# Token-weight transposes in two 64-row halves, own priorities for loads and for every operation

## Chip, cores and metric

The kernel runs on one core of a Trainium2 chip. The metric is the device time of one execution in microseconds (us), median of the runs shown. One execution was also taken by the hardware profiler; its page and trace give where the time goes.

## What is computed

A linear recurrence over the sequence (state of 40 x 40 for each of 4 x 8 batch-heads, 768 steps), and a phase mixer on its output.

```python
# recurrence, for each step t:
y[:, :, t] = einsum('bhd,bhde->bhe', rt, state)
Sa = einsum('bhde,bhe->bhd', state, at)
state = state * wt[:, :, None, :] - einsum('bhd,bhe->bhde', Sa, bt) \
        + einsum('bhd,bhe->bhde', vt, kt)
# mixer on x = y as (batch 4, 768 tokens, 320 channels):
theta = x @ w_theta
zr, zi = x * cos(theta), x * sin(theta)
u = x + einsum('ts,bsd->btd', w_tok_r, zr) + einsum('ts,bsd->btd', w_tok_i, zi)
out = u + maximum(u @ w_ch, 0)
```

## The kernel before

**Tiles.** The sequence is cut into chunks of 128 tokens: 6 chunks in each of 4 batches, 24 tiles `i`. For a tile, the recurrence is done in chunk form for all eight heads at once, with heads padded from 40 to 64 columns so that a pair of heads fills 128.

**Stages of a tile.** `loads` issues five loads on SyncE's queue (w, k, b, a, v, 160 KB each) and, for every second tile, r in two loads. `prep` takes the logarithm of w (ScalarE), its cumulative sum (TensorE) and the exponential of that (`ex`), multiplies k, b and a with it, converts v (GpSimdE, for the first two tiles VectorE and ScalarE) and transposes them on TensorE, ScalarE copying out. `attention_scores` makes three blocks of scores (`spsi`, `sphi`, `slv`), each by eight matmuls of 64 rows into a pair of PSUM banks (line 522), masked by VectorE (line 527). `recurrence` carries the state (`x0`, `nu`, `gt`), `readout` makes a fourth block of scores (`slu`) and the output `x`, `theta` multiplies by w_theta.

**Mixer.** When a batch's six tiles are done, `sines` takes cosine and sine (ScalarE, with a table switch) and GpSimdE multiplies with x into `zr` and `zi`. `mix_row` (line 724) then makes one row block of 128 tokens out of 12 matmuls with 320 columns; VectorE adds x, three transposes, three matmuls with w_ch, VectorE's last step, and a store.

**Token weights.** Both 768 x 768 token matrices are needed transposed. `wtok_block(tb)` (lines 760 to 779), for six blocks of 128 rows, loads the rows of `w_tok_r` and of `w_tok_i` by GpSimdE's queue into `wrow` (two buffers each), and for each matrix runs one TensorE operation `wt` of six 128 x 128 transposes into a single PSUM bank, and one VectorE copy `ewt` into `wtok`.

**Order.** Nothing is issued in program order. Every operation is added to a plan with its engine, an estimated cost, the buffers that it reads and writes, and a tag; `Plan.order` then simulates the engines and at each step issues, for an engine, the ready operation with the lowest score: its priority plus `WAIT` times how much later it could start than the earliest candidate, plus `TSWITCH` for a change of ScalarE's table. The priority is a time for the tile or row (`TIMES`) plus an offset for the kind of operation (`OFF`), line 77. A load of token weights is not planned before its release time (`rel`, in us; the entry 2 + `tb`). TensorE work has a mode, 128 or 64 rows, and the plan adds time for changing it (`INTO64`, `OUTOF64`). The eight PSUM banks are planned too: four as two pairs (cumulative sums and scores), four singly (all else). Buffers `raw_w`, `raw_a`, `raw_kb` and `raw_v` have four copies each, by tile number (lines 287 to 303).

Of the kernel before, what the change touches and what calls it, by code (L numbers as in the profile page):

```python
# [9 lines left out]
FP32 = mybir.dt.float32  # L10
# [10 lines left out]
FREE0 = {"PE": 800.0, "ACT": 2100.0, "DVE": 4400.0, "POOL": 3600.0, "SP": 740.0}  # L21
BANKS = 8
DOUBLE = 4
INTO64, OUTOF64 = 95.0, 120.0
SP_DEPTH = 3600.0

# [7 lines left out]
class Plan:  # L34
# [34 lines left out]
    def link(self):  # L69
        ops = self.ops  # L70
        users = {}
        for o in ops:
            o.succ = []
            o.npre = len(o.pre)
            o.start = o.end = None
            o.banks = None
            o.prio = 1000.0 * (TIMES[o.spec[0]][o.spec[1]] + OFF[o.spec[2]])
            for k in set(o.reads) | set(o.writes):
                if k[0] == "ps":
                    users.setdefault(k, set()).add(o)  # L80
        for o in ops:
            o.soft = set()
            if o.new is not None and not o.loose:
                u = users[o.new[0]]
                o.soft = {p for x in u if x is not o for p in x.pre if p not in u}
                o.soft -= set(o.pre)
            o.npre += len(o.soft)
        for o in ops:
            for p in o.pre:
                p.succ.append(o)  # L90
            for p in o.soft:
                p.succ.append(o)
        return users

    def order(self):
# [44 lines left out]
        while len(out) < n:  # L140
            pick = None
            for e, lst in ready.items():
                if not lst:
                    continue
                te = free[e]
                if e == "SP":
                    te = max(te, dma - SP_DEPTH)
                cand = []
                lo = None
                for o in lst:  # L150
                    t = max(te, est0[o])
                    b = None
                    if o.new is not None:
                        f = find(o)
                        if f is None:
                            continue
                        t = max(t, f[0])
                        b = f[1]
                    if e == "PE" and o.mode != mode:
                        t = max(t, te + (INTO64 if o.mode == 64 else OUTOF64))  # L160
                    cand.append((t, o, b))
                    if lo is None or t < lo:
                        lo = t
                if lo is None:
                    continue
                best = None
                for t, o, b in cand:
                    s = o.prio + WAIT * (t - lo)
                    if e == "ACT" and o.table is not None and o.table != table:
                        s += TSWITCH  # L170
                    if best is None or (s, o.idx) < best[0]:
                        best = ((s, o.idx), t, o, b)
                if pick is None or best[1] < pick[1]:
                    pick = best
# [48 lines left out]
def mm(n):  # L223
    return max(n / 2.4 + 2.5, 25.0)


def tail(n):
# [1 line left out]


OFF = dict(
    ah=-14.03, ch=37.4, cs=-41.22, ea=-6.95, egd=-90.74, egt=-28.2, ekb=21.31, enu=-16.72,
    enut=-11.56, er=-13.46, eth=-25.65, eut=-58.98, ev=17.32, ewt=-9.73, ex=39.26, exp=-63.71,
    ext=-55.21, gd=7.06, gt=16.39, kb=36.69, ln=-32.13, load=-20.04, loadr=-19.62, mlu=62.71,
    mlv=10.93, mphi=44.82, mpsi=69.12, nu=-17.14, nut=12.45, nx=-78.15, oo=13.49, r=35,
    row=38.73, sin=86.83, slu=-15.77, slv=39.92, sphi=-32.67, spsi=-35.87, st=34.23, ta=1.11,
    th=36.56, tkb=-1, tr=0.69, tv=4.86, uadd=-6.95, ut=37.54, v=-26.35, wdma=123.77, wt=37.8,
    x0=-27.08, xt=21.68, y=-40.12, z=24.68)
WAIT, TSWITCH = 435.08, 606442.0
TIMES = dict(  # L240
    tile=[
        -61.22, -38.55, -36.31, -3.78, 3.05, 10.64, 15.26, 42.47, 45.62, 46.74, 54.55, 58.02,
        77.61, 85.12, 102.64, 108.62, 104.48, 129.91, 135.62, 135.6, 150.73, 158.77, 165.34,
        174.78],
    row=[
        47.97, 37.38, 30.67, 33.44, 59.07, 74.74, 77.47, 97.12, 115.85, 115.75, 105.42, 129.53,
        141.42, 164.22, 173.87, 137.03, 124.06, 133.88, 191.51, 200.6, 184.9, 268.51, 279.77,
        212.96],
    rel=[
        -48.76, 34.55, 63.09, 65.85, -76.89, 92.41, 33.44, 33.52])  # L250


@with_exitstack
def kernel(
# [29 lines left out]
    def sb(name, shape, dt, n):  # L284
        return [consts.tile(shape, dt, name=f"{name}_{i}") for i in range(n)]

    raw_w = sb("raw_w", [128, H, D], FP32, 4)
    raw_a = sb("raw_a", [128, H, D], FP32, 4)
    raw_kb = sb("raw_kb", [128, 2, H, D], FP32, 4)
    raw_v = sb("raw_v", [128, H, D], FP32, 4)  # L290
    raw_r = sb("raw_r", [128, 2, 8 * D], FP32, 2)

    def load(i):
        bi, ci = divmod(i, NCH)
        s = i % 4

        def src(ap):
            return ap[bi, :, ci * C:(ci + 1) * C, :].rearrange("h t d -> t h d")
        return ([("raw_w", s), raw_w[s], src(w)],
                [("raw_k", s), raw_kb[s][:, 0], src(k)],  # L300
                [("raw_b", s), raw_kb[s][:, 1], src(b)],
                [("raw_a", s), raw_a[s], src(a)],
                [("raw_v", s), raw_v[s], src(v)])

    ident = consts.tile([128, 128], BF16, name="ident")
    mask_p = consts.tile([128, 1, 128], BF16, name="mask_p")
# [73 lines left out]
    def ps(key):  # L380
        h = plan.home[key]
        return doubles[h[0] // 2] if len(h) == 2 else singles[h[0] - DOUBLE]

# [3 lines left out]
    def add(eng, kind, i, fn, cost, reads=(), writes=(), at="tile", **kw):  # L387
        return plan.add(eng, kind, i, fn, cost, tuple(reads), tuple(writes),
                        (at, i, kind), **kw)
# [23 lines left out]

    def loads(i):
        for key, dst, src in load(i):
            add("SP", "load", i,
                lambda dst=dst, src=src: nc.sync.dma_start(out=dst, in_=src),
                650, [], [key], work=1030)
        bi, ci = divmod(i, NCH)
        if ci % 2 == 0:  # L420
            rr = r[bi, :, ci * C:(ci + 2) * C, :].rearrange(
                "(c g) (t q) d -> c t g (q d)", c=2, q=8)
            s = i // 2 % 2
            for c in range(2):
                add("SP", "loadr", i,
                    lambda c=c: nc.sync.dma_start(out=raw_r[s][:, c], in_=rr[c]),
                    600, [], [("raw_r", s, c)], work=520)

    def natural(t):
        return t.rearrange("p (c g) d -> p g c d", c=2)  # L430

    def paired(t):
        return t.rearrange("p (g c) d -> p g c d", c=2)

    def prep(i):
# [30 lines left out]
        for j, nm in enumerate("kb"):  # L466
# [3 lines left out]
                490 if fast else 864, [("raw_" + nm, s4), kex], [("kb", j, i % NKB)])  # L470
        add("DVE" if fast else "POOL", "ah", i,
            lambda: (nc.vector if fast else nc.gpsimd).tensor_tensor(  # L472
                out=paired(ah)[:, :, :, 0:D], in0=natural(raw_a[s4]), in1=Wi, op=ALU.mult),
            490 if fast else 864, [("raw_a", s4), kex], [("ah", i % 3)])
        copy = nc.scalar.copy if fast else nc.gpsimd.tensor_copy
        add("ACT" if fast else "POOL", "v", i,
            lambda: copy(out=paired(vb)[:, :, :, 0:D], in_=natural(raw_v[s4])),
            460, [("raw_v", s4)], [("v", i % NRV)])
        def tr(kind, kinde, srcs, dst, skeys, dkey, eng):
            p = ("ps", kind, i)  # L480
            n = 4 * len(srcs)
# [278 lines left out]
    def wtok_block(tb):  # L760
        i = 7 + tb
        for nm, ap in (("r", moe_w_tok_r), ("i", moe_w_tok_i)):
            row = wrow[nm][tb % 2]
            add("POOL", "wdma", 2 + tb, lambda row=row, ap=ap: nc.gpsimd.dma_start(
                out=row, in_=ap[tb * 128:(tb + 1) * 128, :]), 580, [],
                [("wrow", nm, tb % 2)], at="rel", work=1240, release=2 + tb)
            p = ("ps", "wt" + nm, tb)

            def go(row=row, p=p):
                t = ps(p).bitcast(BF16)  # L770
                for s in range(NT):
                    nc.tensor.transpose(out=t[:, s * 128:(s + 1) * 128],  # L772
                                        in_=row[:, s * 128:(s + 1) * 128], identity=ident)
            add("PE", "wt", i, go, 6 * mm(128), [("wrow", nm, tb % 2)], [p], new=(p, 1),
                tail=tail(128))
            add("DVE", "ewt", i, lambda nm=nm, p=p: nc.vector.tensor_copy(
                out=wtok[nm][:, :, tb * 128:(tb + 1) * 128],
                in_=ps(p)[:, 0:384].bitcast(BF16).rearrange("p (a b) -> p a b", b=128)),
                550, [p], [("wtok", nm, tb)])

    def mix_rows(bi):
# [71 lines left out]
```

## Time and profile before

| | |
|---|---|
| median of 4 runs | 216.05 us (215.3 to 216.66) |
| profiled execution | 216.33 us |
| its span, first to last instruction | 214.6 us |
| TensorE clock granted | 1.00 throughout |
| token-weight transposes (line 772) | 72 of 128 x 128, from 74.1 to 116.7 us |
| token-weight loads, issued | 66.9 to 107.6 us, in 12 issues |
| first row matmul (line 724) | 76.3 us |
| tile loads | last raw_v issued at 163.1 us |

The longest waits of VectorE, GpSimdE and ScalarE and where they end (engine, line waited for: total us, times, longest):

```profile
POOL kb L468 <- ACT ex L460: 32.8, 9, 15.7
ACT uT L401 <- PE ps_s L625: 17.0, 15, 4.5
POOL zr L706 <- ACT cs L694: 12.8, 6, 5.1
DVE u L734 <- PE ps_s L724: 11.1, 15, 1.3
```

How to read it: PE is TensorE, PEld its weight loads, DVE VectorE, ACT ScalarE, POOL GpSimdE, SP SyncE; a q after the name means the sequencer or queue of that engine. "A <- B" says that A stood idle until B had ended. "ps_s" is a single PSUM bank, "ps_d" a pair. The matmuls of TensorE are pipelined: the duration of one is several times the step from one to the next.

### The profile page before, as it was taken

What the parts mean: (1) busy time and instruction counts of PE and PEld (TensorE: products, weight loads), DVE (VectorE), ACT (ScalarE), POOL (GpSimd) and SP (SyncE); (2) the same over time, 40 slices, a digit from 0 to 9 for tenths busy, and PEclk for the clock granted to TensorE, in tenths of its full rate; (3) what the DMA queues carried; (4) which work ended last, traced back from release to release, by engine and by line L of the source; (5) the groups of instructions that cost most, each with busy time, mean ns of one, the idle gap of its engine ahead of it and who ended that gap; (6) DMA issues with size and microseconds to landing.
All of it is one profiled execution on the core that took longest, in us unless ns stands there. A gap on an engine that the chain in (4) does not pass through costs nothing.

```text
span 214.6 us, 8107 instructions
## 1 busy us (share of the span) xinstructions
PE 195.5 (91%) x3344; PEld 156.4 (73%) x3344; DVE 165.6 (77%) x252; ACT 148.7 (69%) x340; POOL 117.4 (55%) x173
## 2 busy tenths in 40 slices
PE   1478789897999999999999999999999999999993
PEld 1366678685787787888878888787888888777771
DVE  7247798779879798968987889978979899744533
ACT  4266676799989969968788756589967996642101
POOL 5000657488667797967589225386667587150000
PEclk9999999999999999999999999999999999999999
DMA  6999989989898999974999999888999110011222
GB/s 100 212 165 181 165 152 176 185 176 164 176 175 179 185 154 207 192 126 98 210 182 200 175 154 185 144 162 193 159 183 185 34 35 3 0 34 63 91 95 92
DMA packets 134181, 30.82 MB, mean 144 GB/s; under 512 B 125824, under 2 KB 134144, under 8 KB 134144
## 3 DMA queue, kind: packets, MB, share of 16 engines
q1 hardware_dynamic: 131712, 27.54, 65.7%
q0 software_dynamic: 2432, 2.77, 8.7%
q8 instruction: 26, 0.43, 0.8%
q14 instruction: 11, 0.09, 0.2%
HBM read 29.13 MB, written 3.93 MB: 154 GB/s over the span
## 4 chain that ended last, share of the span: by engine, by line
PE 77%; DVE 7%; DMA 4%; issue 3%; POOL 3%; ACT 2%; SPq 1%; POOLq 0%; DVEq 0%; ACTq 0%
PE ps_s L724 19%; PE ps_s L398 13%; PE ps_d L522 11%; PE ps_s L670 9%; PE ps_s L625 4%; DMA raw_a<-in_a_dram 3%; PE ps_s L573 3%; PE ps_s L505 3%; PE ps_s L591 3%; DVE phi L527 2%; PE ps_s L654 2%; DVE psi L527 2%; PE ps_s L772 2%; PE ps_s L652 2%; DMA raw_v<-in_v_dram 2%
## 5 line engine op out<-in xcount | busy, mean ns | idle before, releaser
L468 POOL TENSOR_TENSOR kb<-raw_kb,ex 128x320 bf16<-128x320 f32 x44 | 37.4, 865 | 34.4 <-ACT ex L460 32.8
L724 PE MATMUL ps_s<-zr,wtok_r 128*128 128x320 bf16 x144 | 40.7, 299 | 0.0
L724 PE MATMUL ps_s<-zi,wtok_i 128*128 128x320 bf16 x144 | 40.6, 299 | 0.0
L527 DVE TENSOR_TENSOR psi<-ps_d,mask_p 128x1024 bf16<-128x1024 f32 x24 | 29.2, 1218 | 7.3 <-PE ps_d L522 7.2
L527 DVE TENSOR_TENSOR lamu<-ps_d,mask_p 128x1024 bf16<-128x1024 f32 x24 | 29.3, 1220 | 4.7 <-PE ps_d L522 4.2
L527 DVE TENSOR_TENSOR lamv<-ps_d,mask_p 128x1024 bf16<-128x1024 f32 x24 | 29.0, 1217 | 3.0 <-PE ps_d L522 2.9
L527 DVE TENSOR_TENSOR phi<-ps_d,mask_n 128x1024 bf16<-128x1024 f32 x24 | 29.2, 1215 | 0.7 <-PE ps_d L522 0.6
L472 POOL TENSOR_TENSOR ah<-raw_a,ex 128x320 bf16<-128x320 f32 x22 | 19.0, 865 | 16.0 <-ACT ex L460 7.7
L706 POOL TENSOR_TENSOR zr<-cs,x 128x320 bf16<-128x320 f32 x23 | 17.8, 793 | 12.9 <-ACT cs L694 12.8
L460 ACT ACTIVATE ex<-ps_d 128x648 f32<-128x648 f32 x24 | 17.2, 717 | 7.6 <-PE ps_d L456 4.6
L734 DVE TENSOR_TENSOR u<-ps_s,x 128x320 bf16<-128x320 f32 x24 | 11.7, 488 | 11.2 <-PE ps_s L724 11.1
L401 ACT COPY uT<-ps_s 128x192 f32<-128x192 f32 x24 | 7.7, 321 | 17.1 <-PE ps_s L625 17.0
L706 POOL TENSOR_TENSOR zi<-cs,x 128x320 bf16<-128x320 f32 x23 | 17.7, 792 | 2.1 <-ACT cs L694 2.0
L522 PE MATMUL ps_d<-aT,kbT 64*128 64x128 bf16 x384 | 17.2, 221 | 1.1 <-DVE psi L527 0.5
L401 ACT COPY kbT<-ps_s 128x512 f32<-128x512 f32 x24 | 14.3, 595 | 4.6 <-PE ps_s L398 3.9
L724 PEld LDWEIGHTS <-wtok_r 128*128 128x128 bf16 x144 | 14.0, 97 | 4.5
L724 PEld LDWEIGHTS <-wtok_i 128*128 128x128 bf16 x144 | 14.1, 98 | 3.5
L398 PE MATMUL ps_s<-ident,kb 128*128 128x128 bf16 x192 | 15.4, 223 | 1.3 <-DVE kb L468 1.3
L743 DVE SCALAR_TENSOR_TENSOR oo<-ps_s,u 128x320 f32<-128x320 f32 x24 | 11.5, 486 | 5.2 <-PE ps_s L670 5.2
L654 PE MATMUL ps_s<-kb,lamu 128*128 128x40 bf16 x192 | 15.0, 180 | 0.5 <-DVE lamu L527 0.4
L522 PEld LDWEIGHTS <-kbT 64*128 64x128 bf16 x384 | 11.6, 96 | 5.2 <-issue 2.3
L652 PE MATMUL ps_s<-kb,lamv 128*128 128x40 bf16 x192 | 15.4, 180 | 0.0
(113 smaller groups left out, 556.6 us busy)
## 6 DMA issues: line engine op xcount, KB each, us to landing
raw_w<-in_w_dram SPq DMA_DIRECT2D x24, 160.0 KB, 3.9
raw_kb<-in_k_dram SPq DMA_DIRECT2D x24, 160.0 KB, 4.2
raw_kb<-in_b_dram SPq DMA_DIRECT2D x24, 160.0 KB, 4.2
raw_a<-in_a_dram SPq DMA_DIRECT2D x24, 160.0 KB, 4.2
raw_v<-in_v_dram SPq DMA_DIRECT2D x24, 160.0 KB, 3.9
raw_r<-in_r_dram SPq DMA_DIRECT2D x24, 160.0 KB, 3.7
out_dram<-oo SPq DMA_DIRECT2D x24, 160.0 KB, 2.1
wrow_r<-in_moe_w_tok_r_dram POOLq DMA_DIRECT2D x6, 192.0 KB, 4.3
```

What stands on the lines that cost most here:

```text
L398: nc.tensor.transpose(out=dst[:, c:c + 128], in_=pair(src, g), identity=ident)
L401: nc.scalar.copy(out=out.bitcast(FP32), in_=in_)
L460: add("ACT", "exp", i, lambda: nc.scalar.activation(out=ex, in_=ps(pk).rearrange("p a b -> p (a b)")[:, 512 - DM:512 + DM + 8], func=AF.Ex ...
L468: lambda j=j: (nc.vector if fast else nc.gpsimd).tensor_tensor(out=paired(kb[:, j])[:, :, :, 0:D], in0=natural(raw_kb[s4][:, j]), in1=invW ...
L472: lambda: (nc.vector if fast else nc.gpsimd).tensor_tensor(out=paired(ah)[:, :, :, 0:D], in0=natural(raw_a[s4]), in1=Wi, op=ALU.mult),
L522: nc.tensor.matmul(t[:, q, g, :], lhsT=lhs[rows(q), g * 128:(g + 1) * 128], rhs=rhs[rows(q), g * 128:(g + 1) * 128], start=True, stop=True)
L527: add("DVE", kindm, i, lambda: nc.vector.tensor_tensor(out=dst.rearrange("p a b c -> p (a b) c"), in0=ps(p).rearrange("p a (g c) -> p (a g ...
L652: nc.tensor.matmul(o, lhsT=lamv[:, p, g, :], rhs=kb[:, 0, h, 0:D], start=first, stop=False, skip_group_check=True)
L654: nc.tensor.matmul(o, lhsT=lamu[:, p, g, :], rhs=kb[:, 1, h, 0:D], start=False, stop=True, skip_group_check=True)
L670: nc.tensor.matmul(dst, lhsT=lhs[:, kt, :], rhs=rhs[:, kt, :], start=kt == 0, stop=kt == 2)
L706: nc.vector if fast else nc.gpsimd).tensor_tensor(
L724: nc.tensor.matmul(ps(pk)[:, 0:DM], lhsT=wtok[nm][:, s, j * 128:(j + 1) * 128], rhs=zs[c][:, s], start=n == 0 and c == 0, stop=n == NT - 1 ...
```

## The change

1. `wtok_block`: one TensorE operation for both matrices of a block instead of two. Each 128 x 128 transpose becomes two transposes of 64 rows (partitions 0 to 63 and 64 to 127 of `wrow`), each giving 64 columns; the first half writes one bank of a pair and the second half the other. The operation has mode 64 and takes a pair of banks. The two VectorE copies stay, and now gather 64 columns from each bank.
2. Loads: w, k, b, a and v get a kind each (`lw`, `lk`, `lb`, `la`, `lv`) with its own offset; `raw_a` and `raw_v` have six copies instead of four; the planned issue cost is 600 ns instead of 650.
3. Priorities: every operation gets a correction of its own (`ADJ`, by its number in the plan, 1450 entries); all of `OFF`, `TIMES`, `WAIT` and `TSWITCH` are new; `PSWITCH` is added to the score of a TensorE operation that would change the mode.

```diff
+WTC = 40.0
...
-            o.prio = 1000.0 * (TIMES[o.spec[0]][o.spec[1]] + OFF[o.spec[2]])
+            o.prio = 1000.0 * (TIMES[o.spec[0]][o.spec[1]] + OFF[o.spec[2]] + ADJ.get(o.idx, 0.0))
...
+                    if e == "PE" and o.mode != mode:
+                        s += PSWITCH
...
+    ext=-66.6, gd=9.71, gt=24.29, kb=9.26, la=-21.15, lb=-20.77, lk=-20.66, ln=-93.65,
+    loadr=-19.61, lv=-20.18, lw=-23.04, mlu=71.97, mlv=6.95, mphi=88.14, mpsi=130.68, nu=-17.3,
...
-WAIT, TSWITCH = 435.08, 606442.0
+WAIT, TSWITCH, PSWITCH = 510.2, 393455.0, -8113.0
...
     rel=[
-        -48.76, 34.55, 63.09, 65.85, -76.89, 92.41, 33.44, 33.52])
+        -47, 31.89, 47.14, 65.35, -185.72, 94.98, 65.46, 84.88])
+ADJ = {
+    0: 0.39, 1: -0.66, 2: -0.74, 3: 4.29, 4: -14.65, 5: 17.35, 6: 5.45, 7: -6.34, 8: -5.84,
...
-    raw_a = sb("raw_a", [128, H, D], FP32, 4)
+    raw_a = sb("raw_a", [128, H, D], FP32, 6)
...
-    raw_v = sb("raw_v", [128, H, D], FP32, 4)
+    raw_v = sb("raw_v", [128, H, D], FP32, 6)
...
-                [("raw_a", s), raw_a[s], src(a)],
-                [("raw_v", s), raw_v[s], src(v)])
+                [("raw_a", i % 6), raw_a[i % 6], src(a)],
+                [("raw_v", i % 6), raw_v[i % 6], src(v)])
...
-            add("SP", "load", i,
+            add("SP", "l" + key[0][4:], i,
                 lambda dst=dst, src=src: nc.sync.dma_start(out=dst, in_=src),
-                650, [], [key], work=1030)
+                600, [], [key], work=1030)
...
-            p = ("ps", "wt" + nm, tb)
-
-            def go(row=row, p=p):
-                t = ps(p).bitcast(BF16)
+        p = ("ps", "wt", tb)
+
+        def go():
+            t = ps(p).rearrange("p a b -> p (a b)").bitcast(BF16).rearrange(
+                "p (q c) -> p q c", q=2)
+            for n, nm in enumerate("ri"):
+                row = wrow[nm][tb % 2]
                 for s in range(NT):
-                    nc.tensor.transpose(out=t[:, s * 128:(s + 1) * 128],
-                                        in_=row[:, s * 128:(s + 1) * 128], identity=ident)
-            add("PE", "wt", i, go, 6 * mm(128), [("wrow", nm, tb % 2)], [p], new=(p, 1),
-                tail=tail(128))
-            add("DVE", "ewt", i, lambda nm=nm, p=p: nc.vector.tensor_copy(
-                out=wtok[nm][:, :, tb * 128:(tb + 1) * 128],
-                in_=ps(p)[:, 0:384].bitcast(BF16).rearrange("p (a b) -> p a b", b=128)),
+                    for q in range(2):
+                        c = (n * NT + s) * 64
+                        nc.tensor.transpose(out=t[:, q, c:c + 64],
+                                            in_=row[rows(q), s * 128:(s + 1) * 128],
+                                            identity=ident[rows(q), 64 * q:64 * q + 64])
+        add("PE", "wt", i, go, 12 * WTC, [("wrow", nm, tb % 2) for nm in "ri"], [p],
+            new=(p, 2), mode=64, tail=tail(64))
+        for n, nm in enumerate("ri"):
+            add("DVE", "ewt", i, lambda n=n, nm=nm: nc.vector.tensor_copy(
+                out=wtok[nm][:, :, tb * 128:(tb + 1) * 128].rearrange(
+                    "p s (q c) -> p s q c", q=2),
+                in_=ps(p).rearrange("p a b -> p (a b)").bitcast(BF16).rearrange(
+                    "p (q c) -> p q c", q=2)[:, :, n * NT * 64:(n + 1) * NT * 64].rearrange(
+                    "p q (s c) -> p s q c", c=64)),
                 550, [p], [("wtok", nm, tb)])
```

## The prediction

> **What bounds the kernel now.** I read the page first: busy shares, the 40 slices, the chain; then five-microsecond windows, the chain stretched over the first 60 us, the waits of TensorE, and last the timeline around the token-weight transposes.
>
> ```profile
> span 214.6 us, 8107 instructions
> PE 195.5 (91%) x3344; PEld 156.4 (73%) x3344; DVE 165.6 (77%) x252; ACT 148.7 (69%) x340; POOL 117.4 (55%) x173
> ...
> PE   1478789897999999999999999999999999999993
> ...
> DMA  6999989989898999974999999888999110011222
> ...
> PE 77%; DVE 7%; DMA 4%; issue 3%; POOL 3%; ACT 2%; SPq 1%; POOLq 0%; DVEq 0%; ACTq 0%
> ```
>
> Two parts show. From slice 11 on (some 57 us) PE reads 9 almost everywhere and the chain is PE work, 77% of it. Before that PE has holes while the DMA row is at 8 and 9: a ramp set by the loads. The windows put numbers on it (columns: stretch, then busy us of PE, PEld, DVE, ACT, POOL, clock, DMA share, GB/s).
>
> ```profile
> 10.00:15.00 5.00, 3.72 (x46) 2.91 (x46) 2.35 (x2) 2.77 (x8) 0.00 (x0) 1.00 0.96 155
> ...
> 50.00:55.00 5.00, 4.08 (x85) 2.97 (x82) 4.97 (x5) 4.97 (x11) 4.35 (x7) 1.00 0.97 168
> ...
> 80.00:85.00 5.00, 5.00 (x101) 4.20 (x99) 3.93 (x5) 4.97 (x12) 3.87 (x6) 1.00 1.11 215
> ```
>
> Adding 5 minus PE's figure over such windows: 7.6 us idle in 0 to 10, 6.7 in 10 to 60, 1.3 in 60 to 100, 0.1 from there to 210. In the waits, PE from 60 us on is held three times, 1.1 us in all. So the end moves only by fewer or shorter steps on PE, or by less idle in the ramp. The clock is 1.00 in every window and has no part in it.
>
> One wait in the ramp belongs to a load that the change touches; the chain there (start, us, what):
>
> ```profile
> 51.99 3.62 DMA raw_v<-in_v_dram
> 55.63 0.86 POOL ah L472
> 56.53 0.40 PE ps_s L398 x4
> ```
>
> The steps on PE are read from starts in the timeline, since busy times of pipelined matmuls overlap:
>
> ```profile
> 73.23 0.38 PE L398 MATMUL ps_s<-ident,gt 128*128 128x128 bf16 x4
> 73.55 0.40 PE L522 MATMUL ps_d<-rT,nuT 64*128 64x128 bf16 x8
> 73.95 0.35 PE L573 MATMUL ps_s<-nx,phi 128*128 128x40 bf16 x8
> 74.15 0.49 PE L772 MATMUL ps_s<-ident,wrow_r 128*128 128x128 bf16 x6
> 74.48 0.50 PE L772 MATMUL ps_s<-ident,wrow_i 128*128 128x128 bf16 x6
> ...
> 75.65 0.40 PE L522 MATMUL ps_d<-rT,vT 64*128 64x128 bf16 x8
> 75.98 0.51 PE L772 MATMUL ps_s<-ident,wrow_r 128*128 128x128 bf16 x6
> ```
>
> A 128-column transpose takes (74.48 - 74.15)/6 = 55 ns; a 40-column matmul (74.15 - 73.95)/8 = 25 ns. Eight 64-row halves with their way out take 75.98 - 75.65 = 0.33 us. In the single records of such a group the partner starts 3 or 4 ns after the first half and the next pair 56 ns after that first: 4 x 56 = 0.22, so **leaving the 64-row mode costs 0.10 us**. Entering: 73.55 - 73.23 less 4 x 0.055 is another 0.10. I counted 65 visits to that mode, 34 of one score group and 31 of two: 65 x 0.2 = 13 us of PE's time.
>
> **Part 1, transposes in halves.** Removed: 12 groups of six, 72 x 55 ns = 3.96 us. Added: 72 pairs of halves that move 64 columns each. The trace has no 64-column step. Between 40 columns (25 ns) and 80 columns (35 ns, groups of L591) a straight line gives 31 ns, 34 with the partner's 3; that is the lower bound, 2.45 us, a gain of 1.5. The upper bound is two halves one after another, 62 ns, 4.46 us, a loss of 0.5. I take the lower, because the score halves, which use the same two row ranges and two banks, start 3 ns apart here and so do their weight loads (most pairs of LDWEIGHTS 3 to 4 ns apart).
>
> A rule speaks against this: the Trainium skill, TensorE: Matmul & The Clock Gate, Part 2, has the time of a weight load follow its column count and not its rows, so 144 half loads would cost as much each as the 72 whole ones did. With one load per 25 ns, as the 40-column groups show, serial loads would make a pair 50 ns and the gain only 0.4 us; the 3 to 4 ns between the score pairs' loads say that the two row ranges load side by side.
>
> The group now counts as a 64-row visit. Alone, six of them add 6 x 0.2 = 1.2 us; next to score groups, nothing. The 96 score groups between 10 and 186 us come one per 1.8 us, so I take half: 0.6. **Part 1: -1.5 + 0.6 = -0.9 us**, from -1.5 to +1.7.
>
> Evacuation stays twelve vector copies:
>
> ```profile
> L776 DVE COPY wtok_r<-ps_s x6: 547/556/558, 75.1 to 117.2; 128x768 bf16<-128x768 bf16 x6
> L776 DVE COPY wtok_i<-ps_s x6: 545/552/558, 75.6 to 117.6; 128x768 bf16<-128x768 bf16 x6
> ```
>
> They now read two banks in runs of 64 elements. If that keeps the rate, 0.55 us each; if it falls to the rate of the fp32 rows ((1217 - 488) ns over 704 more elements, about 1.04 ns each) a copy takes 0.95, 12 x 0.4 = 4.8 us more of DVE. DVE is busy 3.2 to 5.0 of 5 us there; PE's queue of row matmuls covers such a delay, so 0, and up to 1.5 if that cover runs out. The group also takes a pair of banks instead of a single one, for about 0.4 + 2 x 0.55 + slack = 1.8 us. There are two pairs; a tile uses them for one cumulative sum and four score groups, some 0.9 + 4 x 1.65 = 7.5 us in the 7.3 us that a tile has (176 us for 24), half of both. Six blocks over 50 us add 11%. PE can go on with single-bank work: 0, up to 1 us. Both matrices must now have landed before the group starts, and everything behind it on PE, in order, waits with it; the two loads are issued 0.6 us apart (66.9 and 67.4) and land in 3.7 to 6.5 us, so an order that counts on the median, 4.8, may lose up to 1.7 once. I take 0, since in the run before no token-weight matmul made PE wait for a load.
>
> **Part 2, loads.** The 144 loads keep their bytes and the one queue; only their order within a tile may change, and the a and v buffers grow from four to six, so such a load may go out two tiles sooner. The queue's table for 10 to 60 us has it at 91% of the engines, so at most 9% of 50 us, 4.5 us, is to be had, and no more than the 6.7 us that PE idles there. What is shown as late is the 3.62 us above and two waits of POOL for raw_v (3.2 us). Two more buffers help only where SyncE waits for a buffer, and by the same token a or v fetched early puts w, k or b back. I take **-0.9**, a quarter of the 3.62; bounds -3.6 and +1.5 (one and a half loads put ahead of a needed one, at 1.07 us: raw_w is issued at 6.66 and, nine tiles on, at 59.57, so 5.9 us a tile of 5.5 loads' bytes).
>
> **Part 3, the order.** 1450 corrections and all kind, tile and release constants are new, so the order on every queue differs, the POOL and SP queues too; it can't be read off the trace. Bounds: if all 96 score groups and six new groups went in pairs there would be 51 visits instead of 65, 14 x 0.2 = -2.8; the remaining idle in the ramp is worth another -2 at most. If every score group went alone, 96 visits, +6.2. Since the waits from 60 us on sum to 1.1 us, little is left outside visits and ramp. I take a third of the -4.8: **-1.6**. The first token-weight pair is released at 47.14 instead of 63.09; what that costs is rival B.
>
> **Sum:** -0.9 - 0.9 - 1.6 = -3.4 us. Against the profiled execution, 216.33 us (its span 214.6 and 1.7 around it), 212.9; the median shown, 216.05, lies 0.28 lower, so **212.7 us**.
>
> **Rivals.** *A, no change:* every new group is a visit of its own (+1.2 - 1.5), the order moves nothing in a PE that is fed anyway: 216.05 - 0.3, with a stretch of DVE delay 0.5: 216.2. For it: from 100 us on PE has no idle to lose. Against: 13 us of switching can be lost by order. *B, slower:* the ramp is the DMA's, and the token weights come into it 16 us earlier. The software queue's 8.7% of the span is 18.7 us for 2.77 MB, so a 0.2 MB matrix takes 1.33 us of all engines. Two of them ahead of tile loads, with 1.1 us of POOL for the two issues (0.59 and 0.54) in front of a tile's kb, ah and v, put attention back 2.65 us where PE has nothing else to do: 216.05 + 2.65 - 0.9 = 217.8. It decides if they land before about 57 us with no row work ready; the sines of tiles 3 to 5, at 69.99, say that the rows can't use them much sooner. Against: a tile's loads are only needed when PE gets there, and from 60 us PE is full. *C, the halves don't overlap:* +0.5 + 1.2 on PE with the other terms kept, 216.05 + 1.7 - 2.5 = 215.3; against it the 3 ns. *D, more than I take:* visits fall to about 51 with the new groups among them, and the ramp gives 3: 216.05 - 1.5 - 2.8 - 3.0 = 208.8.
>
> **From this to the numbers.** About 0.5%, 1.1 us, is what a measurement here tells from no change: 215.0 and 217.1 bound it. Forecast (210.5 to 215.0) 0.52, D (under 210.5) 0.18, A with C 0.13, B and other losses by order 0.17. So faster 0.70, same 0.13, slower 0.17. The likeliest case alone is 210.5 to 215.0; leaving out a tenth at each end, D's lower part and B's upper, gives 208.8 to 217.6.
>
> **What would show it.** Part 1: the step of a pair, 31 to 34 ns between starts against 50 or 62; the twelve copies at 0.55 or 0.95. Part 2: no step of raw_v over a microsecond in the chain before 60 us. Part 3: the number of 64-row visits under 65, PE idle before 60 us under 14.3 us, and the first row matmul sooner than 76.3. B would show as lower PE figures between 45 and 70 us with the token weights in the DMA there. The forecast is wrong if visits rise, or PE from 60 us on is held for more than a few microseconds by DVE or by pairs of banks.

## The result, and the profile after

The changed kernel takes 215.25 us in the median of 54 runs, the kernel before 215.87 in 78 runs beside them: ratio 0.9978, 95% interval 0.9967 to 0.9988, so 0.3 to 0.7 us less. The forecast was 212.7, 3.4 less. The profiled executions are further apart than the medians, 214.81 against 216.33; where that comes from is shown below.

From the page of the changed kernel (span and instructions, busy time, slices, the chain by engine):

```profile
span 213.0 us, 8182 instructions
PE 196.2 (92%) x3416; PEld 155.7 (73%) x3416; DVE 165.6 (78%) x252; ACT 152.9 (72%) x342; POOL 117.6 (55%) x173
...
PE   1589998988979999999999999999999999999993
...
DMA  6998989999989898997899998988996000003122
...
PE 80%; ACT 10%; DVE 4%; issue 2%; DMA 2%; POOL 0%; SPq 0%; DVEq 0%; POOLq 0%; ACTq 0%
```

PE starts sooner (slices 2 to 6) and has a new hole in slice 12, near 60 us. ACT, 2% of the chain before, has 10% now. Two more ACT instructions are one more change of its table and back. Two windows (stretch; busy PE, PEld, DVE, ACT, POOL; clock; DMA):

```profile
10.00:15.00 5.00, 4.15 (x55) 3.11 (x51) 3.69 (x4) 2.98 (x7) 0.00 (x0) 1.00 0.98 170
...
60.00:65.00 5.00, 3.87 (x93) 3.01 (x86) 4.61 (x6) 4.87 (x8) 2.83 (x5) 1.00 0.93 155
```

The first was 3.72 before; the second was 4.96 and is now 3.87. The chain there (start, us, what):

```profile
58.97 0.71 ACT ex L664
59.67 0.26 ACT aT L605
59.94 0.02 issue
59.96 1.28 ACT L898
61.24 0.01 issue
61.25 1.00 ACT cs L898
```

ScalarE loads its sine table (L898) with the recurrence's copies waiting behind it. The first block of token weights runs at that very time:

```profile
61.51 0.35 PE L981 MATMUL ps_d<-ident,wrow_r 64*128 64x64 bf16 x12 [0.34 <-DVE phi L731]
61.68 0.35 PE L981 MATMUL ps_d<-ident,wrow_i 64*128 64x64 bf16 x12
```

Twelve halves, six pairs, start 0.17 us before the next twelve: 28 ns a pair. The copies keep their rate:

```profile
L987 DVE COPY wtok_r<-ps_d x6: 546/547/554, 62.5 to 118.4; 128x768 bf16<-128x768 bf16 x6
```

**PE's account.** Each step from one matmul's start to the next is split into the matmul's own part (the typical steps: 25, 27, 25, 35, 56 and 136 ns for 2, 8, 40, 80, 128 and 320 columns; 28 ns for a score half, 14.5 for a token-weight half), 0.1 us where the row mode changes, and the rest, called stall. In us:

| profiled execution | own part | visits: switching | stall to 20 us | 20 to 60 | 60 to 100 | after |
|---|---|---|---|---|---|---|
| before | 171.1 | 65: 13.0 | 10.2 | 7.5 | 3.3 | 1.9 |
| changed | 169.2 | 69: 13.8 | 9.1 | 6.8 | 3.6 | 2.7 |

The halves take 1.9 off PE's work; four more visits add 0.8; stall falls by 1.8 up to 60 us and rises by 1.1 from there.

### The profile page after: what moved, and what is told of

Read it like the earlier page. It is cut to its first block, busy times and chain, and to the rows that moved or that the text cites. A ratio compares the mean times of both kernels' runs of the same rounds, so it can differ in the third digit from the quotient of the medians.

```text
span 213.0 us, 8182 instructions
## 1 busy us (share of the span) xinstructions
PE 196.2 (92%) x3416; PEld 155.7 (73%) x3416; DVE 165.6 (78%) x252; ACT 152.9 (72%) x342; POOL 117.6 (55%) x173
## 4 chain that ended last, share of the span: by engine, by line
PE 80%; ACT 10%; DVE 4%; issue 2%; DMA 2%; POOL 0%; SPq 0%; DVEq 0%; POOLq 0%; ACTq 0%
PE ps_s L928 19%; PE ps_s L602 15%; PE ps_d L726 11%; PE ps_s L874 9%; PE ps_s L829 4%; PE ps_s L777 3%; PE ps_s L795 3%; PE ps_s L709 2%; PE ps_s L858 2%; PE ps_s L765 2%; PE ps_s L856 2%; PE ps_s L759 2%; ACT ex L664 2%; DMA raw_w<-in_w_dram 2%; PE ps_d L652 1%
## 5 line engine op out<-in xcount | busy, mean ns | idle before, releaser
L676 POOL TENSOR_TENSOR ah<-raw_a,ex 128x320 bf16<-128x320 f32 x22 | 18.9, 862 | 22.6 <-ACT ex L664 13.8
L605 ACT COPY uT<-ps_s 128x192 f32<-128x192 f32 x24 | 7.5, 315 | 14.3 <-PE ps_s L829 12.9
L865 DVE TENSOR_TENSOR x<-ps_s,ex 128x320 bf16<-128x320 f32 x24 | 11.6, 487 | 7.0 <-PE ps_s L858 6.1
L713 ACT COPY rT<-ps_s 128x512 bf16<-128x512 bf16 x24 | 14.2, 594 | 4.0 <-PE ps_s L709 4.0
```

Source lines behind the costliest of these rows:

```text
L605: nc.scalar.copy(out=out.bitcast(FP32), in_=in_)
L676: lambda: (nc.vector if fast else nc.gpsimd).tensor_tensor(out=paired(ah)[:, :, :, 0:D], in0=natural(raw_a[i % 6]), in1=Wi, op=ALU.mult),
L713: add("ACT", "er", i + x, lambda x=x: nc.scalar.copy(out=rT[:, x].rearrange("p (g t q) -> p g t q", g=G, q=8), in_=ps(pr).bitcast(BF16).re ...
```

## Experiments

For most of them the planner's order was written out, so that the issue order and the banks stay as they were and only the edit differs:

```diff
         out.sort(key=lambda o: (o.start, o.idx))
+        out = [ops[i] for i in ORDER]
+        self.home = {("ps",) + k: (v,) if v < 100 else (v - 100, v - 99) for k, v in HOME.items()}
```

Such kernels can be compared matmul by matmul, which is finer than their medians: from the 351st matmul (token-weight ones not counted) to the last, the kernel before takes 177.73 us, and it takes 177.73 again with six buffers. The lag is how much later a matmul starts in one execution than the same matmul in the other. What differs between two executions of one order shows in the lag by 25 us and stays as it is from there.

### 1. Halves undone, order kept

```diff
-                    for q in range(2):
-                        c = (n * NT + s) * 64
-                        nc.tensor.transpose(out=t[:, q, c:c + 64], in_=row[rows(q), s * 128:(s + 1) * 128],
-                                            identity=ident[rows(q), 64 * q:64 * q + 64])
+                    nc.tensor.transpose(out=t[:, n, s * 128:(s + 1) * 128],
+                                        in_=row[:, s * 128:(s + 1) * 128], identity=ident)
```

The two copies read 128 columns at a time again, from one bank for each matrix.

> The changed kernel's order, held fixed operation by operation and bank by bank, with the token weights transposed whole (12 of 128 x 128 per block) in place of 24 halves. Theory 1 (PE time anywhere sets the end): the halves run at 29 ns a pair in the changed kernel's trace, so PE gets 72 x (56 - 29) = 1.9 us more work and loses two of its 69 visits to the 64-row mode (the two that were token weights alone), 0.4: +1.5 us on the changed kernel, about 216.8. Theory 2 (the saving lies where PE waits for something else anyway): no more than 0.4 us above the changed kernel, 215.3 to 215.7.

215.83 us, ratio to the kernel before 1.0004 (0.9990 to 1.0017). Matmul by matmul, the stretch from the 351st to the last is 179.37 us against 178.38 with halves: **0.99 us**, between the theories. (This execution's granted clock is 0.989 on average, but 1.00 from 18.1 to 212.6 us, all over that stretch.) The first block, in the ScalarE hole at 61.5 us, contributes nothing (the lag is -0.29 before and after it); the other five give all of it. PE's account: own part +1.87, switching -0.4, the remaining half microsecond of work taken out of stall. And the new order and loads without the halves are as fast as the kernel before: parts 2 and 3 together are worth 0, within 0.4 us.

### 2. Six buffers, order kept

```diff
-    raw_a = sb("raw_a", [128, H, D], FP32, 4)
+    raw_a = sb("raw_a", [128, H, D], FP32, 6)
```

and the same for `raw_v`, with `i % 6` for the index.

> The kernel before, its order held fixed, with six buffers for raw_a and raw_v in place of four; nothing else. Theory 1 (the buffers alone give nothing, since the order of the loads is fixed and the queue is full): 215.9, within 0.3. Theory 2 (SyncE's waits for a free a or v buffer are what the ramp lost): 1 us or more faster, 214.9 or less.

215.58, ratio 0.9999 (0.9981 to 1.0017): nothing. Its profiled execution ends 0.91 us sooner than that of the kernel before, and all of the 0.91 is there by 10 us and stays to the last matmul. The chain tells from where; its first load ends at 8.52 us in the kernel before and at 7.61 with six buffers, 0.91 sooner:

```profile
2.58 5.94 DMA raw_a<-in_a_dram
...
2.54 5.07 DMA raw_a<-in_a_dram
```

So a profile of either kernel may be off by about a microsecond by how its first loads land.

### 3 and 4. One part under the other's constants

The new `wtok_block` with the old constants, and the changed kernel without its corrections:

```diff
-            o.prio = 1000.0 * (TIMES[o.spec[0]][o.spec[1]] + OFF[o.spec[2]] + ADJ.get(o.idx, 0.0))
+            o.prio = 1000.0 * (TIMES[o.spec[0]][o.spec[1]] + OFF[o.spec[2]])
```

> The new token-weight block alone, under the old constants: the planner makes a new order from the old priorities. Theory 1 (the priorities fit one list of operations only, so a change of the list costs more than the halves give): slower by several us, 218 or more. Theory 2 (part 1 is worth its PE time by itself): 214.0 to 214.5.

> The changed kernel without the 1450 corrections of single operations; its kind, tile and release constants stay. Theory 1 (the corrections carry the order, and the other constants are only right with them): slower by several us, 218 or more. Theory 2 (they are noise around the constants): within 1 us of the changed kernel, 214.3 to 216.3.

233.71 us, ratio 1.0821 (1.0770 to 1.0872), and 229.17, ratio 1.0602 (1.0563 to 1.0640), in four runs each. The constants fit one list of operations. In the first, PE's own part and switching are 183.6 us, as short as the changed kernel's 183.0, and stall is 38.4 instead of 22.2. These two say what a bad order costs, not what the halves or the corrections are worth.

### 5. Fewer loads

```diff
-                lambda dst=dst, src=src: nc.sync.dma_start(out=dst, in_=src),
+                lambda dst=dst, src=src, key=key: None if i > 3 and key[0] in (
+                    "raw_a", "raw_v") else nc.sync.dma_start(out=dst, in_=src),
```

> The kernel before, its order held fixed, without the loads of a and v from the fifth tile on (40 of 144 tile loads; the computation goes on with the a and v of the first four tiles). Theory 1 (the loads set the ramp): 28% fewer bytes in the queue take most of the 12.7 us out of which PE stalls between 10 and 60 us; 205 to 209 us. Theory 2 (the ramp is a chain of ScalarE, VectorE and PE steps, and a fixed order on the other queues): 214 us or more.

215.84, ratio 0.9990 (0.9973 to 1.0008), and 177.74 us from the 351st matmul on: no change, within 0.01. This takes away the prediction's ground, that the loads set the ramp, from 20 us on. The first 20 us, with 10 of some 23 us of stall, are not tested by it: the first four tiles keep their loads, and the chain there starts with one. The chain, in the place where the kernel before has raw_v's 3.62 us:

```profile
46.07 1.28 ACT L863
47.36 0.01 issue
47.37 1.10 ACT cs L863
...
51.92 1.28 ACT L990
...
54.71 0.62 ACT ex L629
...
55.47 0.87 POOL ah L641
56.33 0.05 issue
56.38 0.40 PE ps_s L566 x4
```

The load is gone, and the same transposes start at 56.38 instead of 56.53. But this execution leads by those 0.15 us from 25 us on, so they start as late as before: ScalarE's chain, with two table loads, had been there all along. The load was not even a wait of this place. `ah` reads `raw_a` and `ex`, not `raw_v`; GpSimdE's and ScalarE's rows of the kernel before, then of this one:

```profile
55.62 0.85 POOL L472 TENSOR_TENSOR ah<-raw_a,ex 128x320 bf16<-128x320 f32 x1 [1.04 <-DMA raw_v<-in_v_dram]
54.75 0.73 ACT L460 ACTIVATE ex<-ps_d 128x648 f32<-128x648 f32 x1
...
55.46 0.86 POOL L641 TENSOR_TENSOR ah<-raw_a,ex 128x320 bf16<-128x320 f32 x1 [1.06 <-ACT ex L629]
54.59 0.73 ACT L629 ACTIVATE ex<-ps_d 128x648 f32<-128x648 f32 x1
```

In both, `ah` starts 0.14 us after the end of `ex` (0.13 in experiment 6, where the load is in place and `ex` ends sooner). The load of raw_v landed within these 0.14 us, and the profile, which puts a wait down to what came last, named it.

### 6 and 7. Then without the table loads

```diff
-                    in_=th_t[0][:, js[0]:js[-1] + 1], func=AF.Sin, bias=bias),
+                    in_=th_t[0][:, js[0]:js[-1] + 1], bias=bias,
+                    func=AF.Exp if i == 2 else AF.Sin),
...
+                    table="lnexp" if i == 2 else "trig")
```

> The kernel before, its order held fixed; the sines of tiles 0 to 2 of batch 0 become exponentials, so ScalarE doesn't load tables at 46.2 and 52.1 us (their values are left out). In the chain of the kernel without most loads of a and v, ScalarE's table loads stood where raw_v's 3.62 us stand in the kernel before. Theory 1 (the two waits lie side by side, and either alone is hidden by the other): no change, 215.5 to 216.0. Theory 2 (ScalarE alone sets the ramp there, raw_v was shown only because it came last by little): 0.8 us or more faster, 215.0 or less.

> Both at once: the kernel before, its order fixed, without the table loads at 46.2 and 52.1 us and without the loads of a and v from the fifth tile on (these values are left out). Theory 1 (two waits side by side): only now the end moves, by 1 to 2 us, to 214.0 to 214.9. Theory 2 (ScalarE alone): the same as without the table loads alone. Rival 3 (a longer chain of VectorE and PE lies under both): no change, 215.5 to 216.0.

215.63, ratio 0.9994 (0.9971 to 1.0016), and 215.44, ratio 0.9997 (0.9981 to 1.0012). From the 351st matmul on, 177.48 and 177.49 against 177.73: 0.25 us for the table loads, and not 0.01 more when raw_v goes as well. Rival 3 is nearest: the median lies 0.06 under its range, and the 0.25 us comes with the table loads alone. The chain with both gone:

```profile
47.18 1.21 DVE psi L696
48.39 1.13 DVE phi L696
...
50.67 0.88 DVE lamv L696
...
52.28 1.14 DVE psi L696
...
55.16 0.87 POOL ah L641
56.03 0.05 issue
56.08 0.40 PE ps_s L566 x4
```

This execution leads the kernel before by 0.19 us from 25 to 45 us, so its 56.08 stands for 56.27 there. Two chains reach the same transposes, ScalarE's with its table loads at 56.53 and the one over VectorE's masks at 56.27. Taking out the first was worth the distance to the second, and not the 2.56 us of its two table loads.

### 8. The order of the first loads

31 loads of the kernel before (tiles 0 to 4) in the changed kernel's order, v first, six buffers, all else kept; only entries of `ORDER` differ.

> The kernel before, the order of all other work held fixed, with six buffers for raw_a and raw_v and the first 31 loads (tiles 0 to 4) in the changed kernel's order: v first, then w, b, k, a. Theory 1 (the order of the loads took the stall of the first 20 us down, and it lasts): 214.2 to 214.8, a gain of about 1.2. Theory 2 (what comes sooner at the start is lost again behind a fixed order): 215.3 to 215.9.

216.40, ratio 1.0026 (1.0010 to 1.0042): slower by some 0.5 us, which neither theory had. The first matmul comes at 4.95 us instead of 4.06; by 10 us the lag is 0.2, and it stays there to the end. A likely reading, not tested further: the other engines' order was made for w first.

### 9 and 10. The new ScalarE wait, and the halves without it

The edit of experiment 6 with `i == 5`, on the changed kernel and on that of experiment 1.

> The changed kernel's order, held fixed; the sines of tiles 3 to 5 are replaced by exponentials of the same size, so that ScalarE doesn't load its tables at 60.0 and 69.4 us (2 x 1.28 us less on ScalarE; the values of batch 0 from these tiles are left out). Theory 1 (the new order's wait is ScalarE's chain from 58.5 to 64.3 us, PE at 3.87 of 5 there): PE gets about 1.1 us back between 60 and 65 and the end moves by 0.8 to 1.3, to 214.0 to 214.5. Theory 2 (loads or PE's length set the end, ScalarE is not on the path): 215.0 to 215.5, as the changed kernel.

> The changed kernel's order, fixed, with whole transposes and without ScalarE's table loads at 60.0 and 69.4 us (exponentials for the sines of tiles 3 to 5, values left out). It stands against the run without these table loads that kept the halves (214.34). Theory 1 (ScalarE's chain hid a part of what the halves save): now whole transposes cost 1.0 to 1.5 us, 215.3 to 215.8, instead of the 0.6 with the table loads. Theory 2 (the chain hid only the one block under it): 0.6 to 0.9, 214.9 to 215.2.

214.34, ratio 0.9935 (0.9910 to 0.9960), and 215.46, ratio 0.9988 (0.9974 to 1.0002). The median moved by what theory 1 said, but not in the place that it named:

```profile
60.00:65.00 5.00, 4.02 (x94) 3.02 (x88) 4.61 (x7) 4.07 (x9) 2.88 (x5) 1.00 0.98 161
```

ScalarE is down from 4.87 to 4.07, PE up from 3.87 by 0.15 only. The next chain lay close under it, VectorE's masks again:

```profile
57.83 1.23 DVE lamv L898
...
61.32 1.22 DVE psi L898
...
63.85 1.22 DVE phi L898
```

From the 351st matmul on it takes 177.84 instead of 178.38: 0.54 us less. Of this, 0.35 comes where the two table loads stood (the lag falls by 0.27 at 64 us and by 0.08 at 72); the other 0.19 comes at 202 us, where one wait for ScalarE's copy `uT` is gone, and how that hangs on the edit isn't shown. The rest of the medians' 0.9 is probably scatter of the start, in six runs. Whole transposes take 178.80 here: 0.96 us, as much as with the wait (0.99). So the medians' 1.1 against 0.6 is no sign that ScalarE hid the halves; theory 2's single block gains nothing either, since its place is still a hole.

### 11 and 12. Another order of the same operations

`ORDER` from a search that shifts operations on their engines, with the kernel's own costs (the token-weight group at its measured 0.35 us); the banks and all operations are the changed kernel's.

> The changed kernel with another order of the same operations, from 130 operations on, made so that PE's visits and waits together take less by the kernel's own operation costs (70 visits against 69, fewer waits). Theory 1 (the time over PE's work is the order's): 213.9 to 214.7. Theory 2 (orders this close are all alike on the chip, what sets the end is elsewhere): 215.0 to 215.5.

> The order search carried further from the one that ran at 213.92: the same operations, buffers and banks as the changed kernel, 69 visits to the 64-row mode. By the kernel's own operation costs it is 0.7 us shorter than that one. Theory 1 (the time over PE's work is the order's, and waits, not visits, are what an order can win): 213.0 to 213.6. Theory 2 (the costs are not fine enough to tell orders this close): 213.7 to 214.3.

213.92, ratio 0.9905 (0.9884 to 0.9926), as theory 1 said, and 212.69, ratio 0.9887 (0.9855 to 0.9920), 0.3 us under the range of its theory 1. The two intervals overlap. Both beat both kernels. The windows of the second:

```profile
60.00:65.00 5.00, 4.74 (x103) 3.89 (x102) 4.91 (x7) 4.96 (x11) 4.40 (x6) 1.00 1.02 176
...
100.00:165.00 65.00, 64.96 (x1186) 52.34 (x1184) 54.43 (x69) 53.86 (x120) 44.13 (x62) 1.00 0.83 161
```

The hole at 60 us is mostly filled. Own part and visits are the changed kernel's (169.2; 69: 13.8), stall is 20.4 instead of 22.2: 6.4, 3.2 and 1.7 against 6.8, 3.6 and 2.7 from 20 us on. The first of the two has 70 visits, one more, and is faster: an order won by waits, not by visits.

## Why the prediction was wrong

- **Part 1, -0.9: right**, in part by luck. 0.99 us at fixed order. The saving was 1.9 instead of 1.5, the loss 0.9 instead of 0.6, and the two misses cancel. The step of a pair is 28 to 29 ns, a little under the 31 to 34; a serial 50 did not show, so the halves' weight loads don't add up. Of the 1.9 us saved on PE's work, 0.4 went into two visits of its own and about half a microsecond into stall. The copies at 0.55 us and the pairs of banks cost nothing that the account shows.
- **Part 2, -0.9: this step failed.** "What is shown as late is the 3.62 us above" took a step of the chain as a price, and it was not a wait for that load: `ah`, which follows it there, doesn't read `raw_v` and waited for ScalarE's `ex`. The two waits of POOL for raw_v, 3.2 us, end at 134.3 and 166.2 us, where by the prediction's own count PE idles 0.1 us. Without the load nothing moved, six buffers gave nothing (both within 0.01 us from the 351st matmul on), and the new order of the first loads alone cost 0.2 to 0.5. The bound of +1.5 counts 5.5 loads a tile; there are six (144 for 24 tiles), which makes 0.98 us a load instead of 1.07.
- **Part 3, -1.6: this step failed most.** "I take a third of the -4.8" made a gain out of a bound on gains. Nothing in the trace or the diff said that this order takes any of it. The diff gives no push to fewer visits: `PSWITCH` takes 8113 off the score of a change of mode, and the larger `WAIT` adds (510.2 - 435.08) times the 95 or 120 ns that the plan counts for it, 7100 or 9000, so the two nearly cancel. Two of the signs came, the first row matmul at 72.7 us and 11.5 us of idle PE before 60 us instead of 14.3, and the end did not follow them. The order made 69 visits where I counted on fewer than 65, two of them the halves' own, and while it cut the stall before 60 us by 1.8 (up to 0.9 of that may be the start's scatter), it put the sines of tiles 3 to 5 at 60 us, in front of the recurrence (0.35 to 0.54 us; what their table loads cost at 68.7 us in the kernel before was not run), and stalled 1.1 more after 60. Without the halves, parts 2 and 3 came to 0. The room itself was there: orders of the same operations took 0.9% to 1.1% off the kernel before.
- **The ground, "a ramp set by the loads": wrong from 20 us on.** The DMA row at 9 shows a full queue, not that anyone waits for it; with 28% fewer bytes of tile loads the ramp was the same there. In the first 9 us the chain is a load, raw_a.
- **Rivals.** The outcome is A's, 216.2 expected and 215.25 measured, but A had the visits of the halves eat their gain; it was the order that gave nothing. B did not come: the first token weights went out at 51.4 instead of 66.9 us, and the tile loads still ended earlier (the DMA row is at 0 from slice 32 on). B's sign did, lower PE figures between 45 and 70 us (21.6 of 25 us against 22.7), but the chain there, with and without ScalarE's table loads, holds no load. C is out by the 28 ns. D's size needed an order that this change does not have.

## To carry to other kernels

Before you price a wait, see that the operation that waits reads what the chain names, and what else it reads. A step in the chain of waits is worth only its distance to the next chain; before pricing it, look at what else is busy in the same stretch, and if two engines and the queue are all near full, price it near zero. When a change brings a new order with it, forecast the order at zero with a range on both sides, and only the removed work on the engine that is full with a size. Where the order can be held fixed, compare traces matmul by matmul: here that told 0.25 us apart, which the medians of a dozen runs did not.

## Not expected

With the order fixed, profiled executions agree to 0.01 us from the 351st matmul on (177.73, 177.73, 177.74 in the kernel before and two whose edit had no effect there); they differ by up to 0.9 us, all of it within the first 25 us. Two 64-row transposes of 64 columns in two banks take 28 to 29 ns together, less than the straight line between the 40- and the 80-column steps. A change of ScalarE's table is 1.28 us in every row here, and the sines start 0.01 us after it (61.24 and 61.25 in the chain above). The Trainium skill, ScalarE: Activation LUTs, has about 2.7 us for it in its list of terms; its section What ACT_TABLE_LOAD costs divides that into about 1283 ns of load, as here, and about 1380 ns of a drain that no row shows beside these loads.
